# Top-k attention with an MLP behind it, on one core: the conversion of the second weight matrix, the order at the first block, and some small operations are re-timed

## The chip, the cores and the metric

The kernel runs on one core of a Trainium2 chip. The metric is the device time of one execution in microseconds (us), lower is better. Times of several executions are given as a median with the lowest and the highest; the profile is of one execution, and its span (first to last instruction) is a little shorter than its time.

The engines go by the profile's names: PE is TensorE (matmuls and transposes; PEld is its weight loading), DVE is VectorE, ACT is ScalarE, POOL is GpSimd, SP is SyncE, which here issues nearly all DMAs. Each engine works off its own instructions in the order in which the program lists them, and waits on semaphores for the others.

## The reference

Eight batches of eight heads, a sequence of 576, head width 64, all in float32; the MLP's weights are float64 in memory.

```python
scores = scale * np.matmul(q, k.transpose(0, 1, 3, 2))          # (8, 8, 576, 576)
kth = np.partition(scores, -32, axis=-1)[..., -32:-31]
scores = np.where(scores >= kth, scores, -1000000000.0)
scores = scores - np.max(scores, axis=-1, keepdims=True)
attn = np.exp(scores)
attn = attn / (np.sum(attn, axis=-1, keepdims=True) + 1e-09)
x = np.matmul(attn, v)         # heads side by side: (8, 576, 512)
mu, var = mean and variance of x over its 512 columns
xn = (x - mu) / np.sqrt(var + 1e-06) * g_ln
return x + np.maximum(xn @ w_ch1, 0.0) @ w_ch2      # 512 -> 2048 -> 512
```

So each row of scores keeps its 32 largest entries, and each row of the attention's result goes through a normalised two-layer MLP with a residual.

## The kernel before

**Units and steps.** A *unit* is 128 query rows of both heads of a head pair (two tiles of 128 x 576 scores), or the last 64 rows of both heads as one tile (a "rest" unit). There are 160 units. One long Python loop, `for n in range(END)`, lists the instructions of step n; nothing reorders them. In step n the selection of unit n runs, while neighbours are at other stages:

- `scores(units[n + 2])`: four matmuls (two halves of the keys for each tile) into PSUM, and ACT copies them to SBUF (L376).
- `select(u, 0..3)` on DVE, spread over the step: the row is halved into a larger and a smaller half (`halve`, L416 and L417, at the end of the step before), and four rounds of "eight largest, strike them out" leave the maximum in `u.top` and the 32nd largest in column 7 of `u.thr`. `hi` has two buffers.
- `watch(mk)` for unit n - 1: a tiny subtraction on POOL (L457) that notes in `watched` whether the halving could have lost an entry. Every 16 units `settle_watch` reduces these notes, and `tell` at the end raises a flag by which the whole computation is run again in a safer form. With this data it is not run again.
- `prepare` and `mask` of unit n - 1: ACT scales the threshold and the maximum in place (L450, L451), then for each tile ACT makes a steep ramp from the threshold (L486) and POOL subtracts the scores from it (L489).
- `weigh`: ACT takes the exponential with the row's sum (L497).
- `turn(ex)` for unit n - 1 (up to unit 7) or n - 2: PE transposes the weights (L555), ACT copies them into `pt` (L567); the last columns, the "ends", are transposed and copied apart (L584, L585). From unit 40 on, units that are not the last of their group are turned by DVE and DMAs instead (`move`); three steps later `brings` fetches them into `pt`, and only their ends are transposed, at the start of that step.
- `values(g)` for a group of units two to four steps old: nine matmuls (L609, L616) of values with `pt`, which has one buffer; `take_values` copies the result to `oT` (L624); `place` transposes it (`xo`, L651) and ACT divides by the row sums into `x` (L628).

**The MLP.** When four head pairs of a batch are placed, 256 rows of x are a *block*. `stats` (DVE) centres it, `turn_x` transposes it (L713, ACT's copy L716 into `xT`), and then follow the hidden matmuls (L754) with a ReLU on ACT (L777), and the projection. These go into a list `todo`, and `fill()`, called eight times a step, lists some of them, as many as `slot(n)` says by a planner's costs: up to step `CONVERTING` the difference of DVE's and PE's estimated costs, later an even share of what is left. An item is listed only when the weights that it needs were joined in an earlier step. Block 0 is given at step 9 (`gives_first`), on a quick path: its last group's values, placing and statistics all stand in that step. Block 0 is projected with plain matmuls (L793); all later blocks use seven products in place of eight (L911), which need sums and differences of the halves of w2: `form_pair` makes them on POOL, one pair a step in four steps (L965 to L968), once block 0 is projected.

**The weights.** Float64 is turned into float32 by integer operations, in 32 pieces of 128 x 512: 16 of w1, then 16 of w2. A piece is fetched by SP (`fetch`, into the pool of four `x` buffers, which placed rows and pairs share). `split`: ACT takes the magnitude, the low bits and the sign (L163, L164, L167), for w1 also multiplies the sign by g_ln (L169), and POOL clamps the magnitude (L170). `shift` is one operation on DVE (L173). `join`, a step later: POOL adds and multiplies (L179, L181) into `w1` or `w2`. The sign lies in a borrowed buffer of another pool until the join has read it. `batches[n]` says which pieces step n splits: four before the loop, then two and one by turns up to step 7, which ends w1, then two a step from 8 to 15 for w2. `weights(n, 0)` fetches the next batch and splits the even pieces, `weights(n, 1)` joins the batch before and splits the odd ones. Up to step 6 phase 1 and the shifts stand at the end of the step (`LAZY` is 7), later in its middle.

Of the kernel before, what the change touches and what calls it, by code (L numbers as in the profile page):

```python
# [10 lines left out]
ALU = mybir.AluOpType  # L11
# [18 lines left out]
def compute(  # L30
# [60 lines left out]
    def const(shape, name):  # L91
        return consts.tile(shape, FP32, tag=name, name=name)
# [14 lines left out]
    if doubt is not None:  # L107
        watched = const([P, 34], "watched")
        nc.gpsimd.memset(watched[:], -1.0)
# [12 lines left out]
    class Piece:  # L122
# [26 lines left out]
        def split(self):  # L149
# [6 lines left out]
            else:  # L156
# [5 lines left out]
            size_f = self.size.bitcast(FP32)  # L162
            nc.scalar.activation(size_f, high, AF.Abs)  # L163
            nc.scalar.activation(  # L164
                self.low, self.raw[:, :, 0], AF.Copy, bias=2.0, scale=2.0**-51
            )
            nc.scalar.activation(self.sign[:], high, AF.Sign)  # L167
            if self.i < NF:
                nc.scalar.mul(self.sign[:], self.sign[:], gcol[:, self.c : self.c + 1])  # L169
            nc.gpsimd.tensor_scalar(size_f, size_f, HIGH_MAX, HIGH_MIN, ALU.min, ALU.max)  # L170

# [26 lines left out]
    queue = list(pieces)  # L198
    for n in range(-1, NF):
        count = 4 if n < 0 else 1 + (n + 1) % 2 if n < NF // 2 else 2  # L200
        batches[n], queue = queue[:count], queue[count:]
# [244 lines left out]
    def prepare(u):  # L446

        nt = len(u.tiles)
        u.bias, u.edge = u.top[:, 0:nt, 0], u.thr[:, 0:nt, 7]
        nc.scalar.mul(u.edge, u.edge, STEEP)  # L450
        nc.scalar.mul(u.bias, u.bias, -scale)  # L451

    def watch(u):

        nt = len(u.tiles)
        c = 1 + 2 * (u.i % 16)
        nc.gpsimd.tensor_tensor(  # L457
            watched[:, c : c + nt], u.hi[:, 0:nt, HALF + 7], u.thr[:, 0:nt, 7], ALU.subtract
        )
        if u.i % 16 == 15 or u.i == N - 1:  # L460
            u.ends_watch = True

    def settle_watch():

        for out, first, op in ((0, 0, ALU.max), (33, 1, ALU.min)):
            nc.vector.tensor_reduce(
                watched[:, out : out + 1], watched[:, first : first + 33],
                mybir.AxisListType.X, op,
            )

    def tell():

        w = hpool.tile([P, J * P], FP32, tag="h", name="tell")
        nc.gpsimd.memset(w[:], 0.0)
        nc.vector.tensor_scalar(w[:, 1:2], watched[:, 33:34], -1.0e38, None, ALU.is_le)
        nc.vector.tensor_scalar(w[:, 0:1], watched[:, 0:1], 0.0, None, ALU.is_ge)
        nc.vector.tensor_tensor(w[:, 0:1], w[:, 0:1], w[:, 1:2], ALU.max)
        ps = brief("tell")
        nc.tensor.transpose(ps[:, 0:P], w[:, 0:P], ident[:])
        nc.vector.tensor_reduce(w[0:1, P : P + 1], ps[0:1, 0:P], mybir.AxisListType.X, ALU.max)  # L480
        nc.vector.tensor_copy(doubt, w[0:1, P : P + 1])
# [64 lines left out]
    def turn(u):  # L546
# [25 lines left out]
        def last():  # L572
            ps = turned()
            if u.rest:
                nc.tensor.transpose(ps[0:R, 0:P], u.e[:, 0, JP:S], ident[:])
                nc.tensor.transpose(ps[:, P : 2 * P], u.e[:, 0, JP - R : S], ident[:])
                for h in range(2):
# [4 lines left out]
            else:  # L582
                ends = u.e[:].rearrange("p t n -> p (t n)")[:, JP : JP + P]
                nc.tensor.transpose(ps[:, 0:P], ends, ident[:])  # L584
                nc.scalar.copy(g.pt[:, 2 * J, q0 : q0 + P], ps[:, 0:P])  # L585

        heads = () if u.moved else range(len(u.tiles))
        return [lambda t=t: part(t) for t in heads] + [last]

# [595 lines left out]
    for n in range(END):  # L1185
# [17 lines left out]

        if n:
            for x in due(n):
                scores(x)
        if g:
            values(g)
        if n in brings:
            brings.pop(n)()  # L1210
            turn(at(n - 3))[-1]()
        if quick:
            take_values(g)
        if u:
# [12 lines left out]
        if doubt is not None and at(n - 2) and at(n - 2).ends_watch:  # L1227
            settle_watch()
            if n == N + 1:
                tell()  # L1230
        if mk and doubt is not None:
            watch(mk)
        if early:
            prepare(ex)
            for t in range(2):
                mask(ex, t)
            if n < gives_first - 1:
                weights(n, 0)
            for t in range(2):
                weigh(ex, t)  # L1240
        if not early or n == gives_first - 1:
            weights(n, 0)
# [7 lines left out]
        if g and not quick:  # L1250
            take_values(g)
        if parts:
            parts[0]()
# [27 lines left out]
        if n in ends_due:  # L1281
            fill_ends(ends_due.pop(n))
        if g and not quick:
            place(g)
        if late:
            place_rest(late.job.b, late.job.hp)
        fill(1 if g or late else 0)
        if mk and mk.i >= EARLY:
            weigh(mk, 0)
        fill()  # L1290
# [23 lines left out]
        if u:  # L1314
            select(u, 3)
        if nxt:
            halve(nxt)
# [77 lines left out]
```

## Time and profile before

| | us |
|---|---|
| median of 3 runs | 1632.91 (1632.14 to 1634.82) |
| the profiled execution: its time | 1631.76 |
| its span | 1629.8 |
| PE busy | 1499.9 (92%) |
| DVE busy | 1348.7 (83%) |
| ACT busy | 1108.6 (68%) |
| POOL busy | 1029.1 (63%) |

The mean granted clock of TensorE was 0.969. Busy shares are means over a start with little work for TensorE, a long middle in which attention and MLP run side by side (the last `halve` starts at 1468 us), and an end in which only the MLP is left. In a line of the groups the first number behind the bar is the time that the group's instructions were busy, the second is the mean of one in ns, and then follows the engine's idle time just before them. In a line of waits the three numbers are the total, how often, and the longest. One fp32 matmul of the program stands in the trace as two passes, so that "x8" there are four matmuls.

### The profile page before, as it was taken

What the parts mean: (1) busy time and instruction counts of PE and PEld (TensorE: products, weight loads), DVE (VectorE), ACT (ScalarE), POOL (GpSimd) and SP (SyncE); (2) the same over time, 40 slices, a digit from 0 to 9 for tenths busy, and PEclk for the clock granted to TensorE, in tenths of its full rate; (3) what the DMA queues carried; (4) which work ended last, traced back from release to release, by engine and by line L of the source; (5) the groups of instructions that cost most, each with busy time, mean ns of one, the idle gap of its engine ahead of it and who ended that gap; (6) DMA issues with size and microseconds to landing.
All of it is one profiled execution on the core that took longest, in us unless ns stands there. A gap on an engine that the chain in (4) does not pass through costs nothing.

```text
span 1629.8 us, 27190 instructions
## 1 busy us (share of the span) xinstructions
PE 1499.9 (92%) x7898; PEld 1131.1 (69%) x7898; DVE 1348.7 (83%) x3939; ACT 1108.6 (68%) x3032; POOL 1029.1 (63%) x1473
## 2 busy tenths in 40 slices
PE   2556889899999999999999999999999999999997
PEld 1334646577767677777777777777777777778886
DVE  6866679698999999999999998998899999992000
ACT  6885767678777676777666867677667776764311
POOL 4775875865666676767765747465657666656344
PEclk9867899999999999999999999999999999999999
DMA  8432335312365456545564465546554455432211
GB/s 216 134 99 82 111 80 118 118 57 68 85 167 180 120 148 166 162 145 142 152 189 133 137 152 172 163 116 175 146 171 149 127 155 159 155 98 85 66 39 54
DMA packets 355685, 211.49 MB, mean 130 GB/s; under 512 B 247492, under 2 KB 327880, under 8 KB 355528
## 3 DMA queue, kind: packets, MB, share of 16 engines
q1 hardware_dynamic: 350792, 209.08, 45.2%
q8 instruction: 65, 1.06, 0.3%
q10 hardware_dynamic: 4736, 0.59, 0.2%
q14 instruction: 92, 0.75, 0.2%
HBM read 145.62 MB, written 63.96 MB: 129 GB/s over the span
## 4 chain that ended last, share of the span: by engine, by line
PE 64%; POOL 15%; ACT 12%; DVE 7%; issue 1%; DMA 1%; ACTq 0%; SPq 0%; POOLq 0%; DVEq 0%
PE hps L754 23%; PE ops L911 19%; PE scps L395 8%; POOL e L489 6%; PE av L609 5%; ACT e L486 3%; PE tp L555 3%; DVE m L438 2%; DVE hi L424 2%; PE av L616 2%; ACT sc L376 2%; POOL h L847 1%; ACT e L497 1%; POOL w L181 1%; PE xo L651 1%
## 5 line engine op out<-in xcount | busy, mean ns | idle before, releaser
L489 POOL TENSOR_TENSOR e<-e,sc 128x576 f32<-128x576 f32 x288 | 423.1, 1486 | 441.1 <-ACT e L486 434.0
L754 PE MATMUL hps<-xT,w 128*128 128x256 f32 x2304 | 546.2, 384 | 7.3 <-ACT xT L716 7.3
L754 PEld LDWEIGHTS hps<-xT,w 128*128 128x128 f32 x2304 | 425.0, 192 | 74.1 <-issue 11.5
L438 DVE MAX8 m<-hi 128x8 f32<-128x296 f32 (+1 forms) x1152 | 471.2, 444 | 0.2
L424 DVE MATCH_REPLACE8 hi<-m,hi 128x288 f32<-128x288 f32 (+1 forms) x864 | 377.7, 442 | 0.0
L911 PE MATMUL ops<-w,h 128*128 128x256 f32 x1360 | 322.3, 383 | 1.4 <-POOL h L847 1.4
L911 PEld LDWEIGHTS ops<-w,h 128*128 128x128 f32 x1360 | 251.3, 192 | 40.1 <-issue 5.8
L376 ACT COPY sc<-scps 128x288 f32<-128x288 f32 x576 | 199.1, 407 | 99.3 <-PE scps L395 77.7
L497 ACT ACTIVATE e<-e,m 128x576 f32<-128x576 f32 x288 | 224.8, 781 | 59.5 <-POOL e L489 58.0
L486 ACT ACTIVATE e<-sc,m 128x576 f32<-128x576 f32 x288 | 212.4, 769 | 0.0
L416 DVE TENSOR_TENSOR hi<-sc 128x576 f32<-128x576 f32 (+1 forms) x160 | 135.4, 846 | 59.7 <-POOL watched L457 55.3
L609 PE MATMUL av<-pt,vb 128*64 128x256 f32 (+2 forms) x1088 | 147.2, 412 | 5.9 <-ACT pt L567 4.8
L417 DVE TENSOR_TENSOR lo<-sc 128x576 f32<-128x576 f32 (+1 forms) x160 | 144.1, 901 | 0.0
L555 PE MATMUL tp<-ident,e 128*128 128x128 f32 x576 | 94.0, 291 | 47.0 <-ACT e L497 47.0
L395 PE MATMUL scps<-kT,late_qT 64*128 64x288 f32 (+3 forms) x832 | 129.2, 419 | 8.6 <-ACT pt L567 6.0
L777 ACT ACTIVATE h<-hps 128x512 f32<-128x512 f32 x144 | 85.2, 592 | 66.7 <-PE hps L754 65.7
L911 PE MATMUL ops<-wt,s 128*128 128x256 f32 x544 | 129.3, 381 | 0.0
L555 PEld LDWEIGHTS tp<-ident,e 128*128 128x128 f32 x576 | 76.8, 150 | 69.7 <-ACT e L497 52.3
L528 DVE STREAM_TRANSPOSE sc<-e 128x512 f32<-128x512 f32 x144 | 94.3, 687 | 33.4 <-POOL h L847 16.7
L609 PEld LDWEIGHTS av<-pt,vb 128*64 128x64 f32 x1088 | 72.8, 141 | 67.2 <-issue 15.5
L430 DVE MAX8 hi<-lo 128x8 f32<-128x288 f32 x288 | 117.7, 444 | 0.0
L395 PEld LDWEIGHTS scps<-kT,late_qT 64*128 64x128 f32 (+1 forms) x832 | 72.3, 171 | 61.8 <-issue 18.7
(104 smaller groups left out, 1887.4 us busy)
## 6 DMA issues: line engine op xcount, KB each, us to landing
turned<-sc SPq DMA_DIRECT2D x72, 512.0 KB, 2.9
pt<-turned SPq DMA_DIRECT2D x288, 128.0 KB, 2.7
w<-forms SPq DMA_DIRECT2D x136, 256.0 KB, 3.9
vb<-in_v_dram SPq DMA_DIRECT2D x68, 288.0 KB, 3.9
raw<-in_moe_w_ch_dram SPq DMA_DIRECT2D x32, 512.0 KB, 3.5
kT<-kept SPq DMA_DIRECT2D x36, 288.0 KB, 3.5
kin<-in_k_dram SPq DMA_DIRECT2D x128, 72.0 KB, 2.8
kept<-kT SPq DMA_DIRECT2D x32, 288.0 KB, 3.0
```

The costliest lines, as they stand in the source:

```text
L376: nc.scalar.copy(u.sc[:, t, s * HALF : (s + 1) * HALF], made[s][t][:, 0:HALF])
L395: nc.tensor.matmul(ps[i * R : i * R + ql, o : o + width], qT[r, q0 : q0 + ql], kT[r, k0 : k0 + width], start=True, stop=True,)
L417: nc.vector.tensor_tensor(lo, a, b, ALU.min)
L424: nc.vector.match_replace(x, m[:, t, :], x, LOWEST)
L438: nc.vector.max(m[:, t, :], u.hi[:, t, 0:width])
L486: nc.scalar.activation(u.e[:, t], u.sc[:, t], AF.Relu, bias=u.edge[:, t : t + 1], scale=-STEEP)
L489: nc.gpsimd.tensor_tensor(u.e[:, t], u.e[:, t], u.sc[:, t], ALU.subtract)
L497: nc.scalar.activation(u.e[:, t], u.e[:, t], AF.Exp, bias=u.bias[:, t : t + 1], scale=-scale, accum_out=g.den[:, col : col + 1],)
L555: nc.tensor.transpose(ps[:, c * P : (c + 1) * P], u.e[:, t, c * P + t * R : (c + 1) * P + t * R], ident[:],)
L609: nc.tensor.matmul(av[h * D : (h + 1) * D, 0 : g.nq], vb[:, h * (J + 1) + c, :], g.blocks[:, h, 0 : g.nq // 32, c, :], start=(c == 0), sto ...
L754: nc.tensor.matmul(ps[0][:, side * N : (side + 1) * N], w1[:, c, f * P : (f + 1) * P], self.xT[:, c, 0:N], start=(c == 0), stop=(c == NC - 1),
L911: nc.tensor.matmul(bank[name][:, 0:Q], a(j), rhs, start=first and j == 0, stop=(j == G - 1), skip_group_check=not first,)
```

## The change

- **Batches.** The list of batches gets two empty ones: steps 8 and 9 split nothing, and the 16 pieces of w2 are split in steps 10 to 17. `CONVERTING` grows by two with that. `weights(n, 0)` stands between masks and weighing in all steps up to 8.
- **Factor.** The multiplication of the sign by g_ln moves from ACT to POOL, right behind the clamp, and the clamp is listed right behind the magnitude.
- **Order at the start of a step.** Up to step 9 `values(g)` stands in front of the scores; in step 9 `take_values` does too.
- **Note.** `watch(u)` stands at the end of unit u's own step, behind its last selection and in front of the phase 1 of the weights (up to step 6) and of `form_pair`. `prepare` writes the scaled threshold to column 6 and leaves column 7 for `watch`. `watched` gets two halves, used by turns of 16 units.
- **End copies.** The ends of a moved unit are still transposed at the start of the step, but ACT's copy is listed behind the masks and `take_values`.
- **Placing.** `place` and `place_rest` stand behind one more `fill` and behind `weigh(mk, 0)`.

```diff
@@ split
             nc.scalar.activation(size_f, high, AF.Abs)
+            nc.gpsimd.tensor_scalar(size_f, size_f, HIGH_MAX, HIGH_MIN, ALU.min, ALU.max)
...
             if self.i < NF:
-                nc.scalar.mul(self.sign[:], self.sign[:], gcol[:, self.c : self.c + 1])
-            nc.gpsimd.tensor_scalar(size_f, size_f, HIGH_MAX, HIGH_MIN, ALU.min, ALU.max)
+                nc.gpsimd.tensor_scalar(
+                    self.sign[:], self.sign[:], gcol[:, self.c : self.c + 1], 1.0,
+                    ALU.mult, ALU.mult,
+                )
@@ batches
-    for n in range(-1, NF):
-        count = 4 if n < 0 else 1 + (n + 1) % 2 if n < NF // 2 else 2
+    for n in range(-1, NF + 2):
+        count = 4 if n < 0 else 1 + (n + 1) % 2 if n < NF // 2 else 0 if n < NF // 2 + 2 else 2
@@ prepare, watch
-        u.bias, u.edge = u.top[:, 0:nt, 0], u.thr[:, 0:nt, 7]
-        nc.scalar.mul(u.edge, u.edge, STEEP)
+        u.bias, u.edge = u.top[:, 0:nt, 0], u.thr[:, 0:nt, 6]
+        nc.scalar.mul(u.edge, u.thr[:, 0:nt, 7], STEEP)
...
-        c = 1 + 2 * (u.i % 16)
+        half, c = u.i // 16 % 2, 1 + 2 * (u.i % 16)
         nc.gpsimd.tensor_tensor(
-            watched[:, c : c + nt], u.hi[:, 0:nt, HALF + 7], u.thr[:, 0:nt, 7], ALU.subtract
+            watched[:, half, c : c + nt], u.hi[:, 0:nt, HALF + 7], u.thr[:, 0:nt, 7], ALU.subtract
         )
@@ turn: what last() did becomes a function that transposes and returns the copy
         def last():
-            ps = turned()
...
+            turn_ends(u)()
...
+    def turn_ends(u):
+        q0 = place_of(u) * 32
+        g = u.group
+        ps = turned()
...
+            nc.tensor.transpose(ps[:, 0:P], ends_e, ident[:])
+        def copy():
...
+                nc.scalar.copy(g.pt[:, 2 * J, q0 : q0 + P], ps[:, 0:P])
+        return copy
@@ the loop over steps
-        if n:
-            for x in due(n):
-                scores(x)
-        if g:
+        late_ends = None
+        ahead = due(n) if n else []
+        if g and n <= gives_first:
+            values(g)
+        if quick:
+            take_values(g)
+        for x in ahead:
+            scores(x)
+        if g and n > gives_first:
             values(g)
         if n in brings:
             brings.pop(n)()
-            turn(at(n - 3))[-1]()
-        if quick:
-            take_values(g)
+            late_ends = turn_ends(at(n - 3))
...
-        if mk and doubt is not None:
-            watch(mk)
         if early:
             prepare(ex)
             for t in range(2):
                 mask(ex, t)
-            if n < gives_first - 1:
-                weights(n, 0)
+            weights(n, 0)
             for t in range(2):
                 weigh(ex, t)
-        if not early or n == gives_first - 1:
+        if not early:
             weights(n, 0)
...
         if g and not quick:
             take_values(g)
+        if late_ends:
+            late_ends()
...
+        fill(1 if g or late else 0)
+        if mk and mk.i >= EARLY:
+            weigh(mk, 0)
         if g and not quick:
             place(g)
         if late:
             place_rest(late.job.b, late.job.hp)
-        fill(1 if g or late else 0)
-        if mk and mk.i >= EARLY:
-            weigh(mk, 0)
...
         if u:
             select(u, 3)
+            if doubt is not None:
+                watch(u)
         if nxt:
             halve(nxt)
```

`settle_watch` and `tell` are changed to work on the two halves of `watched`.

More of the change, by code (lines that the diff above doesn't have):

```diff
@@ L107, in compute @@
     if doubt is not None:
-        watched = const([P, 34], "watched")
+        watched = const([P, 2, 34], "watched")
         nc.gpsimd.memset(watched[:], -1.0)
@@ L461, in watch, with settle_watch @@
             u.ends_watch = True
-    def settle_watch():
+            u.half = half
+    def settle_watch(half):
         for out, first, op in ((0, 0, ALU.max), (33, 1, ALU.min)):
             nc.vector.tensor_reduce(
-                watched[:, out : out + 1], watched[:, first : first + 33],
+                watched[:, half, out : out + 1], watched[:, half, first : first + 33],
                 mybir.AxisListType.X, op,
@@ L474, in tell @@
         nc.gpsimd.memset(w[:], 0.0)
-        nc.vector.tensor_scalar(w[:, 1:2], watched[:, 33:34], -1.0e38, None, ALU.is_le)
-        nc.vector.tensor_scalar(w[:, 0:1], watched[:, 0:1], 0.0, None, ALU.is_ge)
-        nc.vector.tensor_tensor(w[:, 0:1], w[:, 0:1], w[:, 1:2], ALU.max)
+        nc.vector.tensor_scalar(w[:, 2:4], watched[:, :, 33], -1.0e38, None, ALU.is_le)
+        nc.vector.tensor_scalar(w[:, 4:6], watched[:, :, 0], 0.0, None, ALU.is_ge)
+        nc.vector.tensor_reduce(w[:, 0:1], w[:, 2:6], mybir.AxisListType.X, ALU.max)
         ps = brief("tell")
@@ L572, in last @@
         def last():
-            ps = turned()
+            turn_ends(u)()
+        heads = () if u.moved else range(len(u.tiles))
+        return [lambda t=t: part(t) for t in heads] + [last]
+    def turn_ends(u):
+        q0 = place_of(u) * 32
+        g = u.group
+        ps = turned()
+        if u.rest:
+            nc.tensor.transpose(ps[0:R, 0:P], u.e[:, 0, JP:S], ident[:])
+            nc.tensor.transpose(ps[:, P : 2 * P], u.e[:, 0, JP - R : S], ident[:])
+        else:
+            ends_e = u.e[:].rearrange("p t n -> p (t n)")[:, JP : JP + P]
+            nc.tensor.transpose(ps[:, 0:P], ends_e, ident[:])
+        def copy():
             if u.rest:
-                nc.tensor.transpose(ps[0:R, 0:P], u.e[:, 0, JP:S], ident[:])
-                nc.tensor.transpose(ps[:, P : 2 * P], u.e[:, 0, JP - R : S], ident[:])
                 for h in range(2):
@@ L582, in last @@
             else:
-                ends = u.e[:].rearrange("p t n -> p (t n)")[:, JP : JP + P]
-                nc.tensor.transpose(ps[:, 0:P], ends, ident[:])
                 nc.scalar.copy(g.pt[:, 2 * J, q0 : q0 + P], ps[:, 0:P])
-        heads = () if u.moved else range(len(u.tiles))
-        return [lambda t=t: part(t) for t in heads] + [last]
+        return copy
     xs, xps, rs, oTr, dr = {}, {}, {}, {}, {}
@@ L1227, in compute @@
         if doubt is not None and at(n - 2) and at(n - 2).ends_watch:
-            settle_watch()
+            settle_watch(at(n - 2).half)
             if n == N + 1:
                 tell()
-        if mk and doubt is not None:
-            watch(mk)
         if early:
```

## The prediction

> **What bounds the kernel now.** I read the page's slices first, then busy time by stretch, then who waited for whom in the stretches with idle time, then the instructions around the longest waits. A "step" is the stretch from one L416 (`halve`) on VectorE to the next; step n ends with unit n's last selection.
>
> ```profile
> PE   2556889899999999999999999999999999999997
> ...
> PEclk9867899999999999999999999999999999999999
> ...
> PE 64%; POOL 15%; ACT 12%; DVE 7%; issue 1%; DMA 1%; ACTq 0%; SPq 0%; POOLq 0%; DVEq 0%
> ```
>
> TensorE is full from the ninth slice on, and 64% of the chain of waits. It is busy 1499.9 of 1629.8 us; the 130 us that it idles can be won.
>
> ```profile
> 20.00:111.00 91.00, 42.42 (x187) 26.34 (x186) 72.83 (x218) 78.20 (x184) 70.69 (x71) 0.83 0.53 145
> 111.00:144.00 33.00, 17.83 (x57) 10.03 (x57) 21.27 (x60) 18.32 (x44) 17.92 (x18) 0.59 0.22 78
> 144.00:213.00 69.00, 59.69 (x278) 42.33 (x278) 41.98 (x133) 56.15 (x136) 52.88 (x54) 0.90 0.37 113
> 213.00:235.00 22.00, 16.53 (x79) 8.84 (x78) 18.45 (x48) 13.54 (x39) 17.97 (x20) 0.92 0.28 63
> 279.00:323.00 44.00, 36.65 (x182) 25.22 (x181) 30.78 (x99) 27.65 (x78) 36.33 (x44) 0.92 0.46 139
> 400.00:800.00 400.00, 386.36 (x2095) 290.02 (x2094) 396.22 (x1156) 293.48 (x837) 270.46 (x387) 0.99 0.53 146
> 800.00:1500.00 700.00, 691.83 (x3724) 534.36 (x3722) 646.96 (x1856) 485.50 (x1357) 444.06 (x676) 1.00 0.51 147
> ```
>
> Columns: length, then busy PE, PEld, DVE, ACT, POOL, granted clock, DMA. Steps 1 to 8 (20 to 111) are full on no engine: ACT 78, VectorE 73, POOL 71 of 91. They are one loop: mask on POOL, exponential on ACT, transposes on PE, copies on ACT, next scores, next mask. Around the first block (111 to 144) everything idles. From 400 to 800 VectorE is full, from 800 on TensorE: there little can be won. So the change is decided before 323 us, and what is won there moves everything behind it.
>
> ```profile
> PE hps L754 <- ACT xT L716: 7.3, 1, 7.3
> ...
> ACT sign L167 <- POOL w L181: 4.8, 1, 4.8
> ```
> ```profile
> 132.14 0.66 ACT L164 ACTIVATE wt<-raw 128x512 f32<-128x512 uint32 x1
> 137.61 0.67 ACT L167 ACTIVATE sign<-raw 128x512 f32<-128x512 f32 x1 [4.82 <-POOL w L181]
> 138.19 1.06 ACT L716 COPY xT<-tp 128x512 f32<-128x512 f32 x2
> ```
>
> These are the waits and ACT's instructions at the first block. The transposed input was ready in PSUM at 131.98 (transpose at 130.87 took 1.11), but its copy stood on ACT behind a weight piece whose sign waited for a buffer that a join frees. The block's first matmul started at 139.30.
>
> ```profile
> DVE hi L416 <- POOL watched L457: 13.5, 4, 5.7
> ACT m L450 <- POOL watched L457: 12.6, 4, 4.7
> ...
> PE xo L651 <- ACT oT L624: 4.0, 2, 3.7
> ```
>
> That is 279 to 323 us, where POOL forms pairs: `watch` stands behind four subtractions of a pair, and both the next `halve` and `prepare` wait for it.
>
> **Pause of the second half.** Batches 8 and 9 (two pieces each) become empty, and 10 to 17 carry the w2 pieces. A piece costs ACT three operations (0.66 + 0.65 + 0.66, issued each 0.57: 1.7 us), POOL one clamp (0.61) and two joins (1.28 + 1.28), VectorE one shift (0.43) and SP one fetch (3.3 us to landing). Nothing is removed, four pieces are two steps later.
>
> *At the first block.* Two pieces stood on ACT between the last exponential (115.78) and the end copy (120.68): 3.4 us go. From there the new order runs values (3.68 + 1.22, clock 0.59), scores (some 3.3 us at that clock), `xo`. Before, six of the eight score passes ran while ACT still copied, so that scores behind the values cost back some 1.7 us; in all `xo` starts some 2.8 us earlier (1.6 of which come from the steps before, next part). From the end of the x products (128.41) to the end of the xT copies (139.24) it took 10.8 us. Left are statistics and transposes (131.98 - 128.41 = 3.6) and a copy (0.6): 4.3, so 6.5 go. **First hidden matmul 9.3 us earlier**; bounds 6.5 (only the stall) and 13 (no scores in the way).
>
> *Steps 10 and 11.* Step 10 has no joins: 4 x 1.28 = 5.1 us leave POOL ahead of the clamp for which VectorE idled 8.40 us at 157.64, and ACT's 2.83 us wait for a join at 154.48 goes. TensorE's hidden work there stays, so I take **4 us** of 5.1; bounds 1 and 5.1.
>
> *Steps 16 to 18* now carry two batches. A loaded step lasts 12.9 us (the clamps that VectorE waited for came at 157.64, 170.56, 183.24: mask, first join, ACT's sign, exponentials, scores, next mask). Unloaded they took 9.33 + 8.64 + 4.53. They are units of one tile, so half the mask (1.4 of 2.8) and half the selection. POOL gets 4 x (0.61 + 2.56) = 12.7 us in a stretch where it idled 22.0 - 18.0 = 4.0: 8.7 us by that; but two projections in step 18 less (built order: 2 in place of 6, 3.4 us of PE) shorten the PE-bound end of the stretch. I take **5 us lost**; bounds 3 and 12.3 (12.9 + 12.9 + 9 against 22.5).
>
> The first block's projection ends a step later, block 1's start and the pairs slip a step. TensorE owes up to 3 us of fill until about step 55; 400 to 800 has 13.6 us of idle PE for it: 0, at most 3 lost if that cover fails.
>
> **The factor.** 16 x 0.722 = 11.6 us leave ACT (0.63 each in its queue), POOL gets 16 `tensor_scalar`s with a column operand.
>
> ```profile
> L688 POOL TENSOR_SCALAR x<-x,less 128x512 f32<-128x512 f32 x30 | 21.4, 712 | 3.1
> ...
> L169 ACT ACTIVATE sign<-sign,gcol 128x512 f32<-128x512 f32 x16 | 11.6, 722 | 0.5
> ```
>
> The nearest row is 0.71 us: 11.4 us. At the start POOL idled 1.8 us between pieces, so five are free, and ACT ends five pieces 3.6 us earlier. Later ones stand behind masks and joins, ahead of the next masks; POOL idled 10.8 of 64 us from 24 to 88, and takes 5 more.
>
> A rule speaks against it. In steps 1 to 8 the row says that the first mask subtraction at 46.77 took 2.24 us where the median is 1.42, just beside L416 and L417. The Trainium skill (SBUF — State Buffer, "SBUF: two separate sides") says that VectorE instructions with two SBUF inputs and GpSimd hold one port pair exclusively, the loser waiting for the whole instruction. By it each factor could meet that pair of instructions (1.4 us), an estimate of 16 x 1.4 = 22 us lost on POOL, by the row 0.8 us now and then.
>
> **Values in front of scores, up to step 9.** On steps 3, 5 and 7 the loop now has the nine value matmuls (2.12 + 0.70) between end copy and scores, where they ran in PE's idle time: some 1.7 us lost each after ACT's shorter piece. Against that, `watch` no longer stands behind joins: VectorE's waits in steps 1 to 8 (3.39 + 2.80 + 0.74 + 3.53) go, and ACT's 5.07 us wait at 35.33, of which POOL's joins keep some 3. Following the loop through, 3.8 us are won by step 1, and 1.6 are left at the last early mask (112.18). Bounds: 4 lost (three times 1.7 with nothing won) to 5 won.
>
> **Note, placing, end copies.** `watch` in front of the pair: `prepare` writes another column, so that mask follows pair without the 1.12 us round trip and 0.20, three to four steps, in a stretch where POOL is the bound: **4 us won**; bounds 0 and the 7.35 us that PE idles in 279 to 323. Placing one projection later covers PE's waits for oT (13 us from 330 to 1510, 8.7 from 600 on); what is queued behind the later x products on ACT is the next head copy and exponential, 0.93 us, in an engine 70% busy. The 72 end copies (0.28 each) leave ACT's front, where they waited 76 us for their transposes; masks start earlier, which nothing full waits for. Together **2 us won**; bounds 3 lost (0.93 us met on a few dozen PE-bound steps) and 8 won (PE's idle after 800). The two halves of `watched`, the memset and `tell` cost nothing: TensorE works until 1630, `tell` runs at 1513; without that cover some 0.3 us.
>
> **Sum.** 9.3 + 4 - 5 + 4 + 2 = 14.3 us off the profiled execution's 1631.8 (span 1629.8): 1617.5. Its own time lies 1.1 under the median of 1632.9, so I say 1618.
>
> **Rivals.**
> - *Given back* (0.18): steps 16 to 18 cost 12 and POOL is as full as before where the pairs are formed (gain 1): 9.3 + 4 - 12 + 1 + 2, about 4 us: 1628. For it: POOL is busy 18 of 22 us there already. Against: these units have one tile.
> - *Slower* (0.18): the early loop. The values in front of scores cost more than they should, because each holds scores, copies and next mask, and the loop, not VectorE, is the bound; it decides once steps 3, 5, 7 and 9 lose more than 14.3 together, 3.6 each on top of what is counted. At 5 each (values, wait for the end copy and for the PSUM buffer that oT's copy frees) it is 6 us slower: 1639. For it: PE waited 47 us for exponentials there. Against: ACT loses a piece's factor in the same loop.
> - *More* (0.08): the early steps win 5, the forming 7, the rest 8: 1605.
> - *Does nothing* (0.06): steps 10 to 18 end when they did, since the same pieces must be joined before the projection: 1632. Against: the matmuls ready first are the hidden ones, which need w1 alone.
>
> My forecast has 0.50. Range 1607 to 1634: it leaves out most of "more" and most of "slower". On its own the forecast holds 1611 to 1624. A measurement of this kernel can tell about 0.2% (3.3 us). Faster 0.74 (forecast, most of given back, more), same 0.08, slower 0.18.
>
> **What would show it.** Right: first hidden matmul near 130 us, ACT without a wait in front of the xT copies, no wait of `halve` for `watched` in steps 1 to 8 and in the pair stretch, steps 16 to 18 some 27 us long, 400 to 1500 with the same busy shares. Wrong: mask starts in steps 3 to 8 later than before, factors of 1.3 us or more on POOL, or steps 16 to 18 over 34 us.

## The result and the profile after

The changed kernel takes 1622.86 us (median of 4 runs, 1620.08 to 1624.3) against 1633.55 of before: a ratio of 0.9933 with an interval of 0.9916 to 0.995, 10.9 us faster. The profiled execution took 1620.08, its span is 1618.2. The forecast was 1618. The sum was nearly right, but most of its terms were not, and the profile already shows it. First the page's slices and its chain:

```profile
PE   2547779899989899999999999999999999999997
...
PEclk9778889999999999999999999999999999999999
...
PE 68%; DVE 14%; POOL 10%; ACT 5%; issue 1%; DMA 1%; DVEq 0%; POOLq 0%; SPq 0%; ACTq 0%
```

POOL's share of the chain fell from 15% to 10% and ACT's from 12% to 5%, VectorE's rose from 7% to 14%. VectorE is also busy longer, 1390.1 us in place of 1348.7, and 39.6 of these 41.4 us lie in the two instructions of `halve`, first before, then after:

```profile
L416 DVE TENSOR_TENSOR hi<-sc 128x576 f32<-128x576 f32 (+1 forms) x160 | 135.4, 846 | 59.7 <-POOL watched L457 55.3
L417 DVE TENSOR_TENSOR lo<-sc 128x576 f32<-128x576 f32 (+1 forms) x160 | 144.1, 901 | 0.0
```
```profile
L420 DVE TENSOR_TENSOR lo<-sc 128x576 f32<-128x576 f32 (+1 forms) x160 | 166.7, 1042 | 0.0
L419 DVE TENSOR_TENSOR hi<-sc 128x576 f32<-128x576 f32 (+1 forms) x160 | 152.4, 953 | 14.6 <-POOL watched L460 9.5
```

On 128x576 each of them took at most 0.76 us where POOL ran nothing beside it but the tiny note, and up to 1.98 us where it ran something larger; of the 256, 146 ran so before and 191 after. So VectorE's wait for the note fell by 45.8 us (55.3 to 9.5), and its halving took 39.6 us longer.

Busy time by stretch, with the columns of the prediction's table (length, then PE, PEld, DVE, ACT, POOL, clock, DMA):

```profile
20.00:111.00 91.00, 41.44 (x173) 25.83 (x171) 75.78 (x206) 63.94 (x155) 80.56 (x77) 0.84 0.52 141
111.00:144.00 33.00, 23.05 (x99) 15.91 (x99) 25.75 (x72) 19.87 (x55) 18.53 (x19) 0.72 0.10 31
144.00:213.00 69.00, 56.53 (x261) 38.27 (x261) 47.68 (x141) 53.10 (x128) 50.27 (x52) 0.88 0.37 116
213.00:235.00 22.00, 13.94 (x74) 7.36 (x70) 13.10 (x35) 19.17 (x49) 19.71 (x21) 0.92 0.54 142
279.00:323.00 44.00, 38.86 (x206) 28.40 (x205) 43.56 (x117) 28.54 (x80) 42.26 (x43) 0.92 0.38 107
400.00:800.00 400.00, 388.35 (x2120) 294.81 (x2118) 398.53 (x1167) 294.51 (x847) 273.14 (x395) 0.99 0.53 149
800.00:1500.00 700.00, 697.33 (x3758) 542.44 (x3755) 655.78 (x1848) 481.75 (x1358) 465.68 (x672) 1.00 0.51 146
```

At the first block (111 to 144) TensorE does 5.2 us more, before it and in 144 to 235 it does less (41.44 against 42.42, and 70.47 against 76.22). Summed from the start to 400 us, TensorE idles 100.5 us, against 98.4 before: all that the first block won is gone by then. The gain of the whole kernel comes from 500 us on. In 800 to 1500 TensorE idles 2.7 us in place of 8.2. The waits from 460 to 1410 us say why; first before:

```profile
ACT pt L585 <- PE tp L584: 62.2, 42, 2.7
...
ACT m L450 <- POOL watched L457: 27.4, 22, 4.1
DVE hi L416 <- POOL watched L457: 14.8, 11, 4.9
...
PE xo L651 <- ACT oT L624: 11.2, 17, 1.8
```

and the same view after (L667 and L640 are `place` and `take_values`, L460 is `watch`, L592 the ends' transpose):

```profile
ACT e L490 <- PE tp L592: 40.9, 26, 2.6
POOL watched L460 <- DVE m L441: 29.5, 26, 3.3
...
DVE hi L419 <- POOL watched L460: 2.7, 2, 2.4
...
PE xo L667 <- ACT oT L640: 0.2, 1, 0.2
```

TensorE's wait for oT is gone, and so is ACT's for the note. POOL now waits for VectorE's last selection with the note, where before ACT waited for POOL. ACT still waits 40.9 us for the ends' transposes, now in front of the mask's ramp (L490) and no longer at the copy (62.2 before).

The first block itself, TensorE's instructions of after in time order (start, duration, instruction, in brackets the idle time before and its releaser):

```profile
128.60 0.44 PE L667 MATMUL xo<-ident,oT 128*128 128x128 f32 x2
131.74 0.63 PE L729 MATMUL tp<-ident,x 128*128 128x128 f32 x4 [2.70 <-DVE x L698]
133.25 1.11 PE L729 MATMUL tp<-ident,x 128*128 128x128 f32 x4 [0.89 <-DVE x L698]
135.04 4.59 PE L770 MATMUL hps<-xT,w 128*128 128x256 f32 x10 [0.68 <-ACT xT L732]
```

From `xo` to the first hidden matmul it is 6.4 us, and the last 7.3 us wait for a copy has become 0.68. But `xo` itself starts later than the prediction had it, since step 9 begins at 118.2 us where it began at 111.0.

### The profile page after: what moved, and what is told of

It reads as the page before. It is cut to its first block, busy times and chain, and to the rows that moved or that the text cites. A ratio compares the mean times of both kernels' runs of the same rounds, so it can differ in the third digit from the quotient of the medians.

```text
span 1618.2 us, 27185 instructions
## 1 busy us (share of the span) xinstructions
PE 1493.6 (92%) x7898; PEld 1132.9 (70%) x7898; DVE 1390.1 (86%) x3939; ACT 1090.9 (67%) x3016; POOL 1081.8 (67%) x1489
## 4 chain that ended last, share of the span: by engine, by line
PE 68%; DVE 14%; POOL 10%; ACT 5%; issue 1%; DMA 1%; DVEq 0%; POOLq 0%; SPq 0%; ACTq 0%
PE hps L770 25%; PE ops L927 21%; PE scps L398 8%; PE av L625 7%; DVE m L441 4%; DVE hi L427 4%; POOL e L493 3%; PE tp L559 2%; PE av L632 2%; DVE lo L420 2%; DVE hi L419 2%; POOL w L184 2%; DVE hi L433 1%; PE tp L729 1%; ACT sc L379 1%
## 5 line engine op out<-in xcount | busy, mean ns | idle before, releaser
L770 PEld LDWEIGHTS hps<-xT,w 128*128 128x128 f32 x2304 | 423.0, 191 | 66.9 <-issue 11.6
L490 ACT ACTIVATE e<-sc,m 128x576 f32<-128x576 f32 x288 | 212.8, 770 | 42.9 <-PE tp L592 42.9
L420 DVE TENSOR_TENSOR lo<-sc 128x576 f32<-128x576 f32 (+1 forms) x160 | 166.7, 1042 | 0.0
L419 DVE TENSOR_TENSOR hi<-sc 128x576 f32<-128x576 f32 (+1 forms) x160 | 152.4, 953 | 14.6 <-POOL watched L460 9.5
L625 PE MATMUL av<-pt,vb 128*64 128x256 f32 (+2 forms) x1088 | 152.1, 419 | 5.9 <-ACT r L644 4.3
L398 PE MATMUL scps<-kT,late_qT 64*128 64x288 f32 (+3 forms) x832 | 124.9, 411 | 17.0 <-ACT pt L571 9.5
L625 PEld LDWEIGHTS av<-pt,vb 128*64 128x64 f32 x1088 | 77.0, 144 | 67.4 <-issue 14.2
```

What stands on the lines that cost most here:

```text
L398: nc.tensor.matmul(ps[i * R : i * R + ql, o : o + width], qT[r, q0 : q0 + ql], kT[r, k0 : k0 + width], start=True, stop=True,)
L420: nc.vector.tensor_tensor(lo, a, b, ALU.min)
L490: nc.scalar.activation(u.e[:, t], u.sc[:, t], AF.Relu, bias=u.edge[:, t : t + 1], scale=-STEEP)
L625: nc.tensor.matmul(av[h * D : (h + 1) * D, 0 : g.nq], vb[:, h * (J + 1) + c, :], g.blocks[:, h, 0 : g.nq // 32, c, :], start=(c == 0), sto ...
L770: nc.tensor.matmul(ps[0][:, side * N : (side + 1) * N], w1[:, c, f * P : (f + 1) * P], self.xT[:, c, 0:N], start=(c == 0), stop=(c == NC - 1),
```

## The experiments

Kernels of one group ran on the same chip, beside before. The letters of the parts: P pause (batches), F factor, V values in front of the scores, N note, E end copies, L placing later. "N, E and L" are the three re-timings. Ratios are to before, one part in a thousand is 1.6 us. Where a "450th" or a "600th" hidden matmul is named, the MLP's matmul records (hidden and projection) are counted in order of time. Times from a trace are of one execution, and that of before (1631.76) lies 1.8 us under the median of 1633.55, so that steps compare to 1 or 2 us.

### First group: start against middle

*The three edits of the start* (P, F and V) on before:

```diff
+    for n in range(-1, NF + 2):      # two empty batches
...
+                nc.gpsimd.tensor_scalar(self.sign[:], self.sign[:], gcol[:, self.c : self.c + 1], ...
...
+        if g and n <= gives_first:
+            values(g)                # in front of scores
...
+            weights(n, 0)            # between masks and weighing in step 8 too
```

> Before with the pause, the factor on POOL and the values in front of the scores (the three edits of the start), without note, end copies and placing. Prediction on record: 9.3 + 4 - 5 = 8.3 us faster, 1625. Theory A (the gain is made in the long middle, 500 to 1400 us, by the small re-timings; the start gives back what it wins by 400 us): within 4 us of before, 1630 to 1637, with the first hidden matmul 3 to 5 us earlier and the 450th hidden matmul at the time of before. Theory B (the start's gain is carried on and only hidden for a while behind work that TensorE owes): 7 to 11 us faster, and it shows between 500 and 1400 us.

Measured: 1637.61 us, ratio 1.0018 (1.0007 to 1.0029). The start edits alone cost 3 us. The first hidden matmul came 1.3 us earlier (137.97), less than the 3 to 5 of theory A, and the 450th came 6.6 us later. Theory B falls; theory A has the sign, but the start does not only give back, it loses.

*The three re-timings* (N, E and L) on before:

```diff
-        if mk and doubt is not None:
-            watch(mk)
...
+                watch(u)             # behind select(u, 3)
...
-            turn(at(n - 3))[-1]()
+            late_ends = turn_ends(at(n - 3))
...
+        if late_ends:
+            late_ends()
...
+        fill(1 if g or late else 0)  # and weigh(mk, 0), then place
```

The note has its column 6 and the two halves of `watched` with it.

> Before with note, end copies and placing alone; the start is that of before. Prediction on record: 4 + 2 = 6 us faster, 1627. Theory A: 9 to 13 us faster, 1620 to 1624, with TensorE's waits of xo for oT gone and its idle time from 800 to 1500 us down from 8 to 2 us. Theory B: 0 to 4 us faster.

Measured: 1618.13 us, 0.9903 (0.9888 to 0.9917): 15.8 us faster than before, and faster than the changed kernel by 0.3% (the two intervals just touch). TensorE's waits for oT after 460 us fell from 11.2 to 1.8. This is more than theory A asked.

*Placing alone:*

```diff
-        if g and not quick:
-            place(g)
-        if late:
-            place_rest(late.job.b, late.job.hp)
         fill(1 if g or late else 0)
         if mk and mk.i >= EARLY:
             weigh(mk, 0)
+        if g and not quick:
+            place(g)
+        if late:
+            place_rest(late.job.b, late.job.hp)
```

> Before with placing one projection later alone. Theory A with the placing as its cause: TensorE's waits of xo for oT after 460 us (11.2 us) go to below 1, and the time falls by 8 to 11 us, to 1622 to 1625. If the end copies or the note are the cause: within 3 us of before, though the waits for oT go, because another wait of TensorE takes their place. Prediction on record: within placing and end copies 2 us together.

Measured: 1624.68 us, 0.9946 (0.9933 to 0.9958), 8.8 us. One line of waits from 460 to 1410 us and one of busy time:

```profile
PE xo L651 <- ACT oT L624: 4.2, 5, 1.1
```
```profile
800.00:1500.00 700.00, 695.52 (x3748) 539.66 (x3747) 641.03 (x1853) 484.27 (x1358) 441.73 (x677) 1.00 0.51 147
```

Seven us of the 11.2 went (4.2 stay, not "below 1"), and TensorE is busy 3.7 us more in 800 to 1500. Of its other waits only one grew, that of the values for `r` (2.3 us in place of 0.6). One more `fill` now stands in front of `place`, so TensorE has MLP matmuls to do while the copy to oT runs.

*End copies alone:*

```diff
-            turn(at(n - 3))[-1]()
+            late_ends = turn_ends(at(n - 3))
...
+        if late_ends:
+            late_ends()              # behind mask(mk, 1) and take_values
```

> Before with the later copies of the ends alone. ACT's 62 us of waits for the transposed ends after 460 us go in any case. If these delayed masks that VectorE's end of step depends on, VectorE's waits for exponentials (9.7 us, in the sum over a tile's parts) go and the time falls by 3 to 8 us. If they cost nothing, as the prediction had it, within 2 us of before, 1631 to 1635.

Measured: 1631.2 us, 0.9982 (0.9974 to 0.9991), at the edge of what can be told from no change. The wait at the copy went, but half of it only moved. In the waits from 460 to 1410 us it now stands in front of the ramp:

```profile
ACT e L486 <- PE tp L588: 32.3, 21, 2.6
```

The tile `e` of the attention's weights has two buffers, so the ramp of unit n - 1 writes over what the ends' transpose of unit n - 3 reads, and must wait for it wherever the copy stands. VectorE's wait for exponentials did not go either (12.0 us, before 9.7), so the mechanism of the first expectation is not it. Its trace ends no earlier than that of before (span 1630.2 and 1629.8). The three us by the medians can't be placed.

### Second group: each part of the start on top of the re-timings

The step that each time stands for in this table is read from the starts of `halve`, the "hidden" column is the start of the first hidden matmul (us, one execution each):

| kernel | step 9 begins | hidden | step 12 | step 16 | step 19 | step 30 | ratio |
|---|---|---|---|---|---|---|---|
| before | 111.0 | 139.30 | 160.3 | 212.6 | 235.1 | 338.0 | 1 |
| after | 118.2 | 135.04 | 151.2 | 205.5 | 238.3 | 340.1 | 0.9933 |
| N, E, L | 110.1 | 137.28 | 158.0 | 209.3 | 232.3 | 331.9 | 0.9903 |
| N, E, L and pause | 109.9 | 126.67 | 142.9 | 197.0 | 229.7 | 331.5 | 0.9894 |
| N, E, L and factor | 112.1 | 137.83 | 158.3 | 209.6 | 233.0 | 332.7 | 0.9907 |
| N, E, L and values | 116.0 | 144.38 | 165.7 | 218.6 | 242.0 | 341.7 | 0.9956 |
| after without V | 112.9 | 128.46 | 144.8 | 199.3 | 232.0 | 332.4 | 0.9908 |
| after, V in step 9 alone | 112.7 | 129.27 | 146.2 | 200.8 | 234.1 | 335.5 | 0.9906 |
| N, E, L, pause of one step | 110.8 | 131.42 | 152.1 | 202.6 | 233.4 | 332.5 | 0.9867 |

*With the pause* (in the diff of batches, and `weights(n, 0)` between masks and weighing in step 8 too):

```diff
-        count = 4 if n < 0 else 1 + (n + 1) % 2 if n < NF // 2 else 2
+        count = 4 if n < 0 else 1 + (n + 1) % 2 if n < NF // 2 else 0 if n < NF // 2 + 2 else 2
```

> Note, end copies and placing with the pause added (no factor, no values in front). Prediction on record: the pause wins 9.3 + 4 - 5 = 8.3 us against the three alone (1618.1): 1610. Theory C (the pause only moves the load: what steps 9 to 11 win, steps 12 to 18 lose, as in the run of the three start edits where steps 16 to 18 grew from 22.5 to 33.1 us): 1615 to 1619. Theory D (the pause itself costs): 1621 or more.

Measured: 1615.42 us, 0.9894 (0.9877 to 0.9911), inside the interval of the three alone. What the pause does at the first block is large. TensorE's wait at the first block with the three alone, and with the pause:

```profile
137.28 2.93 PE L767 MATMUL hps<-xT,w 128*128 128x256 f32 x6 [7.32 <-ACT xT L729]
```
```profile
126.67 3.78 PE L767 MATMUL hps<-xT,w 128*128 128x256 f32 x8 [0.68 <-ACT xT L729]
```

It starts 10.6 us earlier, and step 12 begins 15.1 us earlier. Then, by the table, steps 12 to 15 take 2.8 us more, 16 to 18 take 32.7 in place of 23.0, and 19 to 29 take 2.2 more: at step 30 0.4 us are left. Theory C holds: the load is moved, and the steps from 12 on give it all back.

*With the factor on POOL:*

```diff
-                nc.scalar.mul(self.sign[:], self.sign[:], gcol[:, self.c : self.c + 1])
+                nc.gpsimd.tensor_scalar(
+                    self.sign[:], self.sign[:], gcol[:, self.c : self.c + 1], 1.0, ALU.mult, ALU.mult,
+                )
```

> Note, end copies and placing with the factor on POOL added. Prediction on record: nothing either way, 1617 to 1619. If the factor is what delays the early steps (POOL as the loop's bound): the last early mask and the first hidden matmul come 3 to 8 us later, 1621 to 1626.

Measured: 1616.93 us, 0.9907 (0.9891 to 0.9922): nothing either way. But it is not free at the start, where step 9 begins 2.0 us later. The groups by shape, first the joins of w1 with the three alone, then joins and factors with the factor on POOL (busy, mean ns of one):

```profile
L181 POOL TENSOR_TENSOR w<-size,sign 128x512 f32<-128x512 f32 x16 | 22.8, 1425 | 1.3
```
```profile
L184 POOL TENSOR_TENSOR w<-size,sign 128x512 f32<-128x512 f32 x16 | 25.4, 1588 | 1.3
...
L170 POOL TENSOR_SCALAR sign<-sign,gcol 128x512 f32<-128x512 f32 x16 | 14.1, 879 | 2.5 <-ACT sign L168 1.4
```

*With the values in front of the scores:*

```diff
-        if n:
-            for x in due(n):
-                scores(x)
-        if g:
+        ahead = due(n) if n else []
+        if g and n <= gives_first:
+            values(g)
+        if quick:
+            take_values(g)
+        for x in ahead:
+            scores(x)
+        if g and n > gives_first:
             values(g)
```

> Note, end copies and placing with the values in front of the scores up to step 9 added. Prediction on record: three times 1.7 lost in steps 3, 5 and 7 and 1.7 in step 9, less what is won by the quick path in step 9: 1619 to 1624. If it is what delays the early loop in the run of the three start edits (steps 4 and 6 were 2.4 and 1.5 us longer there, step 9 began 8.6 us later): 1623 to 1627. If the loop hides it: 1617 to 1619.

Measured: 1624.56 us, 0.9956 (0.9942 to 0.997): 8.7 us lost against the three alone. TensorE in steps 3 to 5, first with the three alone:

```profile
51.47 0.42 PE L589 MATMUL tp<-ident,e 128*128 128x128 f32 x1
51.82 2.29 PE L395 MATMUL scps<-kT,qT 64*128 64x288 f32 x8
54.04 2.92 PE L622 MATMUL av<-pt,vb 128*64 128x256 f32 x16
56.88 0.70 PE L629 MATMUL av<-pt,ends 128*128 128x256 f32 x2
60.92 1.11 PE L556 MATMUL tp<-ident,e 128*128 128x128 f32 x4 [3.34 <-ACT e L498]
```

and with the values in front:

```profile
52.59 0.42 PE L589 MATMUL tp<-ident,e 128*128 128x128 f32 x1
52.95 2.95 PE L622 MATMUL av<-pt,vb 128*64 128x256 f32 x16
55.82 0.70 PE L629 MATMUL av<-pt,ends 128*128 128x256 f32 x2
56.45 1.24 PE L395 MATMUL scps<-kT,qT 64*128 64x288 f32 x8
63.55 1.11 PE L556 MATMUL tp<-ident,e 128*128 128x128 f32 x4 [5.85 <-ACT e L498]
```

The scores start 4.6 us later where the ends' transpose before them came 1.1 later. The values had run in idle time in front of the next transposes; there the idle time is now longer (5.85): the copies of the scores stand on ACT in front of the ramp and the exponential, so these come later too. Against the three alone the first exponential that is listed in step 3 loses 1.5 us, that of step 5 another 1.7 and that of step 7 another 1.8. By the medians of the two runs the loss is 6.4 us, by the ratios 8.7.

*The note alone:*

```diff
-        if mk and doubt is not None:
-            watch(mk)
...
             select(u, 3)
+            if doubt is not None:
+                watch(u)
```

with column 6 for the scaled threshold and the two halves of `watched`.

> Before with the note at the end of its own step alone. Prediction on record: 4 us won where pairs are formed (279 to 323 us) and some in the early loop: 1627 to 1631. What is left of the three together after placing and end copies alone (15.7 - 8.8 - 2.9 by the medians measured): 4 us, 1629.5. In the run of the three the hidden matmuls ran 9 us ahead between 320 and 440 us and lost 3 of them by 500; if that is the note's doing, the same is seen here and the time falls by 4 to 7 us, 1627 to 1630.

Measured: 1622.41 us, 0.9942 (0.9927 to 0.9957), 9.5 us. Hidden matmuls are 8.7 us ahead of before at the 450th (372.6 us) and 5.5 at the 750th (490.8), much as in the run of the three. So placing and note each give some 9 us alone, but only 15.8 together with the end copies: they overlap. One place of it is seen in the waits after 460 us: with the note alone TensorE's waits for oT are already down from 11.2 to 6.3.

### Third group: the causes

*V in step 9 alone*, on the changed kernel:

```diff
-        if g and n <= gives_first:
+        if quick:
             values(g)
-        if quick:
             take_values(g)
...
-        if g and n > gives_first:
+        if g and not quick:
```

> The changed kernel with the values in front of the scores in step 9 alone; steps 1 to 8 have the scores in front again. Theory E (the loss of the values in front lies in steps 3, 5 and 7, where nine value matmuls now hold the scores, their copies and the next mask): step 9 begins 5 to 7 us earlier than in the changed kernel, and the time falls from 1622.9 to 1616 to 1618. Prediction on record: three times 1.7 us, 1617.8. Theory F (the loss is in step 9): less than 2 us under the changed kernel.

Measured: 1616.86 us, 0.9906 (0.9891 to 0.9921); step 9 begins at 112.7 in place of 118.2. Theory E holds: three steps lose 5.5 us together, a mean of 1.8.

*The changed kernel without V:* the order of the loop is that of before, the rest that of after.

```diff
-        if g and n <= gives_first:
-            values(g)
-        if quick:
-            take_values(g)
         for x in ahead:
             scores(x)
-        if g and n > gives_first:
+        if g:
             values(g)
```

> Note, end copies, placing, pause and factor: the changed kernel without the values in front. Theory E: 1613 to 1617, some 7 us under the changed kernel, with the first hidden matmul near 127 us. If the factor costs where the pause has moved the load (POOL fuller in steps 1 to 8): over 1618. Against the same without the factor (1615.4) the prediction on record has 0.

Measured: 1616.92 us, 0.9908 (0.9893 to 0.9924). The values in front in step 9, where the quick path was to win by them, are worth nothing (0.9906 against 0.9908; the first hidden matmul is 0.8 us later with them).

*Column 6 alone:*

```diff
-        u.bias, u.edge = u.top[:, 0:nt, 0], u.thr[:, 0:nt, 7]
-        nc.scalar.mul(u.edge, u.edge, STEEP)
+        u.bias, u.edge = u.top[:, 0:nt, 0], u.thr[:, 0:nt, 6]
+        nc.scalar.mul(u.edge, u.thr[:, 0:nt, 7], STEEP)
```

> Before, with only one piece of the note's edits: the scaled threshold goes to column 6, so that ACT no longer waits for the note; the note itself stays behind the joins and pairs, and the next halving still waits for it. If ACT's wait (27.4 us after 460 us, 12.6 in 279 to 323) was what cost: 7 to 11 us faster, as the whole note, 1622 to 1626. If VectorE's wait was it (10.5 us in steps 1 to 8, 13.5 in 279 to 323, 12.9 in 323 to 500): within 3 us of before. Prediction on record: each gives a part of 4 us.

Measured: 1624.28 us, 0.9946 (0.9933 to 0.996), 8.8 us of the 9.5 that the whole note gives. The wait in the pair-forming stretch, 279 to 323 us, was 13.5 us for VectorE and 12.6 for ACT before; here:

```profile
DVE hi L416 <- POOL watched L457: 3.9, 2, 3.0
```

ACT's is gone, and VectorE's fell by 9.6 though the note still stands behind the pair on POOL. Before, POOL did pair, note, and then idled for ACT's scaling and ramp; with the column free, ACT scales while POOL forms the pair, the mask follows at once, and the next pair and note come earlier. That ACT's half of this reuse of a column set the pace is what the run shows, since VectorE's half was left as it was. VectorE itself won nothing by it: over the whole run its wait for the note fell by 28.6 us (55.3 to 26.7), and its halving took 29.1 us longer (279.5 to 308.6). The time is won on TensorE, whose waits for oT after 460 us fell from 11.2 to 7.5.

*A pause of one step* (N, E, L and batch 9 alone empty; the even piece of step 8 is split between masks and weighing):

```diff
-        count = ... 0 if n < NF // 2 + 2 else 2
+        count = ... 0 if n in (NF // 2 + 1, NF + 1) else 2
```

> Note, end copies, placing and a pause of one step: step 8 splits two pieces again, step 9 none, and the w2 pieces end in step 16 in place of 17. Theory C (the pause of two steps is given back by the two more loaded steps 16 to 18, 9.7 us longer than without it, while the first hidden matmul won 10.6): the first hidden matmul stays 8 to 11 us earlier than without a pause, one loaded step less wins 4 to 5 us back, 1609 to 1613 against 1615.4 with the pause of two. If the piece in step 8 delays the first block as much as before: 1616 to 1619.

Measured: 1609.83 us, 0.9867 (0.9852 to 0.9883) and the fastest of all, 0.66% under the changed kernel by the ratios. The number is that of theory C, the place is not: the first hidden matmul is 5.9 us earlier than without a pause, not 8 to 11, by the table its steps 9 to 18 take 122.6 us against 119.8 with the pause of two, and its 600th hidden matmul is 1.5 us later (429.6 against 428.2). At the 750th it is 3.8 us ahead (486.9 against 490.7), so it wins between 430 and 490 us: busy time in 450 to 465, with the pause of two and of one,

```profile
450.00:465.00 15.00, 10.65 (x46) 8.00 (x43) 14.83 (x42) 7.58 (x22) 6.25 (x10) 0.77 0.35 112
```
```profile
450.00:465.00 15.00, 14.08 (x81) 9.98 (x80) 14.83 (x41) 10.48 (x30) 7.56 (x12) 1.00 0.36 111
```

and two of TensorE's lines at the hole, with the pause of two, then the one that answers the second with the pause of one:

```profile
454.19 0.66 PE L726 MATMUL tp<-ident,x 128*128 128x128 f32 x4 [3.44 <-POOL x L701]
...
456.67 5.33 PE L924 MATMUL ops<-w,h 128*128 128x256 f32 x12
```
```profile
454.49 2.76 PE L924 MATMUL ops<-w,h 128*128 128x256 f32 x12
```

A block's transposed input waits for POOL's centring while TensorE has nothing else to do, and the granted clock of the 15 us falls to 0.77. With the pause of one TensorE still had projection work there, and the same wait is 0.35 us. The hole of 3.44 and the 2.57 us that the 12 projection passes take longer behind it come to 6.0, the size of the gain (5.6 us by the medians, 4.4 by the ratios). Why the work lies otherwise is open: that the planner spreads it because `CONVERTING` is one step less is likely, but was not tried apart.

## Why the prediction was right, point by point

The time was 1622.9 for 1618, inside the forecast's own range of 1611 to 1624, and only just nearer to it (4.9 us) than to the rival "given back" at 1628 (5.1). It came out right by luck, because errors of both signs met. The runs, each with one part more than the last, give by their ratios: the three re-timings 15.8 us won, the pause 1.5 won, the factor 2.3 lost, the values in front 4.1 lost, together the 10.9 (for each of the last three the intervals of the two runs overlap). The sum had 6 for the re-timings and 8.3 for the start; the start measured some 5 lost.

- **First hidden matmul 9.3 earlier: 4.3 measured** (139.30 to 135.04). The part that the pause has in it was, if anything, too small: 10.6 by the pair of runs, within the bounds of 6.5 and 13, and the stall of 7.3 us went. The part of the early steps failed: 1.6 was to be left at the last early mask, and that came 5.9 us later (112.18 to 118.11), step 9 7.2 us later. The runs take that apart: -1.1 from the re-timings with the pause (111.0 to 109.9), +3.0 from the factor (to 112.9), +5.3 from the values (to 118.2).
- **Values in front, 1.7 lost in each of steps 3, 5 and 7: right** (1.5, 1.7 and 1.8). What failed is the gain set against it. Of the 3.8 us that the note was to win early, 3.2 are there at step 2 (32.1 against 35.3 with the three), but only 0.9 of them reach step 9. The values in front cost 8.7 us on top of the three and some 4 in the changed kernel (0.9933 against 0.9908; by the medians 5.9).
- **The factor neutral: right in the end, wrong at the start.** A factor took 0.88 us on POOL (predicted 0.71; half of them at most 0.70, the longest 1.66), and the joins beside it took 2.6 us more. Weighed again: 16 factors at 0.70 would be 11.2 us, 14.1 were measured, so 2.9 and 2.6 make 5.5 us of POOL over the row. The Trainium skill (SBUF — State Buffer, "SBUF: two separate sides") has GpSimd and VectorE instructions with two SBUF inputs hold one port pair in turn, the second waiting for the whole of the first; the prediction worked this out as an estimate of 22 us. In the run with the factor alone nine of the 16 took 0.69 to 0.70 us, three that ran beside a halving took 1.09, 1.33 and 1.66, and four that began beside `shift` took 0.93. So some meet, for a quarter of that price on POOL, and the time of this run did not move. The estimate also left out the other side, VectorE as the one that waits, which the halving shows (0.76 us at most by itself, up to 1.98 beside larger work of POOL); but the factor did not add to that (323.4 us of halving with it, 328.1 without).
- **Steps 10 and 11, 4 won: 4.5** between the first hidden matmul and the start of step 12 in the run with the pause (20.7 to 16.2 us), so that step 12 begins 10.6 + 4.5 = 15.1 us earlier. **Steps 16 to 18, 5 lost: 9.7** there and 10.3 in the changed kernel (22.5 to 32.8), within the bounds of 3 and 12.3; the reason for taking the low side, two projections fewer, did not show. Steps 12 to 15 and 19 to 29, which the sum had at nothing, lost 5.0. So 14.7 of the 15.1 us are gone at step 30, and the pause, 6.7 us in the sum without the early steps' share, is worth nothing that can be measured: for it the rival "given back" was right.
- **Note, 4 won: 9.5**, above the bound of 7.35. The bound was TensorE's idle time in one stretch, but the wait was in two: ACT's 27.4 us for the note after 460 us went too, and the hidden matmuls gain another 6 us there (5.5 ahead at the 750th, 11.6 at the 3600th). Most of it is the spare column (8.8 us by itself), which the sum had as some 1.3 us a step in three to four steps.
- **Placing and end copies, 2 won: 6.4** on top of the note (0.9903 against 0.9942), placing alone 8.8. This term is mis-sized by its reading: TensorE's idle time after 800 was named as the bound of 8, and then little of it taken, on the word that from 400 us on "little can be won". For the end copies "masks start earlier" did not hold: 32.3 of ACT's 62.2 us of waits for the transposed ends moved to the front of the ramp. The three re-timings were 6 us of the sum, and they are 15.8.
- The signs of being right: no wait of ACT in front of the xT copies for a join came, and next to none of `halve` for the note in steps 1 to 8 (1.2 us for 10.5) and in the pair stretch (0.4 for 13.5). The first hidden matmul near 130 us (135.04), steps 16 to 18 near 27 us (32.8) and equal busy shares from 400 to 1500 (TensorE does 7.5 us more there) did not. Of the signs of being wrong one came in full: from step 3 to step 8 the masks start 3.8 to 5.9 us later than before. Two of the 16 factors took over 1.3 us.
- The rival "slower" had the right place. It needed 14.3 us more on steps 3, 5, 7 and 9; the last early mask was 7.5 us off, the factor's share of it included, and the re-timings paid for it.

## What to carry to other kernels

Price a small wait on a full engine by its sum over the whole run, not by its length: 17 waits of TensorE, the longest 1.8 us, were worth as much (7 of their 11.2 us went, and 8.8 us of the time) as the stall of 7 us that the eye falls on, and the gain was kept to the end, where the stall's was not. Work that is moved out of a hole lands in later steps; look at what is full there before counting the gain. And where an operation is written in place, ask who must read the old value first: one more column of memory was worth 8.8 us. And when a wait goes, look whether the instructions behind it have become longer: VectorE's busy time grew by nearly what its wait for the note fell.

## What the runs showed that was not expected

- Gains of parts that touch different engines do not add: 9.5 (note), 8.8 (placing) and 2.9 (end copies) make 21.2, and together they give 15.8; the gap of 5.4 is little more than the four intervals together leave open (some 4, an estimate from their half-widths). The part of the change that was put at the start, by itself, made the kernel slower (1.0018).
- One batch moved by one step (a pause of one for two) changes TensorE's work more than 200 us after the last of the moved pieces, from 10.65 to 14.08 us in the 15 us after 450, and the time by 0.27% (0.9867 against 0.9894).
- Where TensorE ran out of work for 3.4 us, the granted clock of the stretch was 0.77, in the same stretch without that hole 1.00. In detail, with the pause of two:

```profile
455.05:461.88 6.83, 6.12 (x17) 5.05 (x18) 6.73 (x17) 2.58 (x6) 4.21 (x5) 0.50 0.22 76
550.63:557.45 6.82, 6.16 (x19) 5.04 (x20) 6.79 (x20) 1.17 (x2) 2.08 (x4) 0.50 0.21 80
717.88:721.29 3.41, 3.21 (x16) 1.71 (x16) 3.34 (x8) 2.41 (x8) 1.93 (x5) 0.50 0.00 0
```

  The clock was half for 6.8 us behind the hole, and 12 projection passes took 5.33 us there in place of 2.76, so that such a hole costs more than its own length. The Trainium skill (TensorE: Matmul & The Clock Gate, "Part 1: The HAM clock gate") has the clock fall to one half after an idle window of some 3.4 us. The hole of 3.44 us agrees with it; the other two lines stand at holes of 2.88 and 2.02 us, so that in this trace the clock fell at shorter holes too.
